# Attention scores on both halves of the partitions, low parts on VectorE, and a matrix of its own for leftover rows

## The chip, the cores and the metric

The kernel runs on one core of a Trainium2 chip. The metric is device time in microseconds (us) of one execution. TensorE (PE) does the matmuls; its weight loads are listed apart as PEld. VectorE is DVE, ScalarE is ACT, GpSimd is POOL, and SyncE (SP) only issues DMAs here.

## The reference

Three layers in a row, in float32, with batch 8, 8 heads, 576 rows, head size 64, 32 memory slots, model width 512 and MLP width 1024:

```python
# attention over a memory of 32 slots, per batch and head
a = softmax(phi, axis=2)                      # 576 x 32
k_m, v_m = a.T @ k, a.T @ v                   # 32 x 64
attn = softmax(q @ k_m.T / 8)                 # the scores: 576 x 32
x = heads_side_by_side(attn @ v_m)            # 576 x 512

# first MLP, with a token shift
x_prev = x shifted down by one row
xk, xr = mu_k*x + (1-mu_k)*x_prev, mu_r*x + (1-mu_r)*x_prev
x = sigmoid(xr @ w_r) * (relu(xk @ w_k)**2 @ w_v)

# second MLP, with a spatial gate
h = relu(x @ w_in); u, v = h[:, :512], h[:, 512:]
v_s = w_spatial @ layer_norm(v) + b_spatial[:, None]
out = (u * v_s) @ w_out
```

The weights reach the kernel as the bits of 64-bit floats and are turned into float32 on the chip.

## The kernel before

**Precision.** Every operand of a large matmul is split into a high part of a shorter float type (an ACT copy) and a low part (a subtraction), and a product is three products: high by high, low by high, high by low (`three`, `gemm`, the matmul at line 95). `split` does it with ACT and DVE (lines 102 and 103); `load_f64`, which brings in a weight chunk, converts its bits (lines 117 to 134) and then splits it with ACT and POOL (lines 140 and 141). A chunk is 128 partitions by 1024 words, 512 KB. The scores alone are plain float32 matmuls, of two instructions each.

**Attention.** `att_step(i)` handles four heads of one batch, so there are 16 steps. A step normalises phi with the transposed maximum (line 222), forms k_m and v_m for the four heads on 32 partitions each (line 233), transposes k_m to 64 partitions (`kmp`, line 267; copied at 268) and computes the scores: for each half of the 576 rows (288, `HB`) a PSUM bank, 4 or 5, with the four heads on 32 output partitions each (line 278). Both operands lie on partitions 0 to 63. A DVE transpose (line 282) takes each half out. Between the halves stands a `yield`. In steps 2 to 15 both halves are normalised together; steps 0 and 1 take one half at a time.

**Order of the work.** The program is written as generators that are advanced by hand. Steps 0 and 1 of attention, the loads and the eight chunks of w_k (`w`) follow the string `ORDER`: A, C, K, Q are phi transposed, phi, keys with values, and queries of step 0; B, D, L, R those of step 1; a lower-case letter is the late half of the queries; `a` and `b` advance the steps; I and M are small constants. Then 16 half batches (`i` in `2 * B`) of the first MLP run; within the first of them `FIRST_BLOCK` brings in the chunks of w_r and w_v. `pump()` after each block of matmuls advances the attention of later batches, and from half batch 14 on `w_in_steps`, which loads w_in and w_out and forms the seven sums that the second MLP's block products use. A tile that is asked for again under the same tag waits until its last reader is done. The compiler's scheduler may start work earlier than its place in the program, but each engine's instructions run in one fixed order, and a DMA waits its turn in SP's queue.

**Between the MLPs.** Each chunk of the first MLP's result is stored to DRAM (`x2d[b]`, line 669) and read back by `load_x2` (lines 553 and 559) as four quarters of 512 rows, whose differences (`minus`, line 548, on POOL) and splits (`put`) feed the second MLP. The products are block products with seven in place of eight (`Group.step`, steps 1, 6, 2, 7, 5, 3, 4): a result is either copied out by ACT (steps 1 and 5, lines 754 and 762) or added by DVE (line 751), and some sums are formed on POOL. `uv(n)` does the u and v products of one batch; as 576 is 512 + 64, the 64 leftover rows of the eight batches are gathered into one more matrix of 512 rows, `uv(B)`. For it `load_x2(B)` reads four pieces from the eight matrices for each quarter. Its steps are advanced by `turn()` during `uv(0)`.

Of the kernel before, what the change touches and what calls it, by code (L numbers as in the profile page):

```python
# [33 lines left out]
ORDER = "AICKMBwwDQwLqwrRaaawaaabbbabaabbwbbwbw"  # L34
# [6 lines left out]
def kernel(  # L41
# [40 lines left out]
    x2d = [dram.tile([128, KC, S], F32, name=f"x2d{b}", tag=f"x2d{b}") for b in range(B)]  # L82
# [25 lines left out]
    def load_f64(src, wh=None, wl=None, raw=None):  # L108
# [32 lines left out]
        nc.gpsimd.tensor_tensor(out=wl, in0=v, in1=wh.bitcast(F32), op=ALU.subtract)  # L141
# [27 lines left out]
    def att_space(f, q, o, n, w, r):  # L169
# [11 lines left out]
        ns.kmT = cut(f, 128)[0:64]  # L181
# [6 lines left out]
        ns.km = cut(n, 64)  # L188
# [10 lines left out]
    def operands(i):  # L199
        b, g = divmod(i, G)  # L200
        sp = space(i)
        return (sp.pT, phiT[b, g]), (sp.ph, phin[b, g]), (sp.kv, kv1[b, g]), (sp.q, qT[b, g])
# [7 lines left out]
    def att_step(i):  # L210
# [30 lines left out]
        nc.vector.tensor_scalar(out=km, in0=kvp[:, 0:64], scalar1=rs, scalar2=None, op0=ALU.mult)  # L241
# [24 lines left out]
        kmp = bank(n_small)[0:64, 0:128]  # L266
# [5 lines left out]
        for halves in ((0,), (1,)) if i < 2 else ((0, 1),):  # L272
            bl = slice(halves[0] * NBLK // 2, (halves[-1] + 1) * NBLK // 2)
            sl = slice(halves[0] * HB, (halves[-1] + 1) * HB)
            for hf in halves:
                sc = bank(4 + hf)[:, 0:HB]
                for j in range(HG):
                    nc.tensor.matmul(  # L278
                        out=sc[32 * j:32 * j + 32, :], lhsT=kmT[:, 32 * j:32 * j + 32],
                        rhs=q[:, j, hf * HB:(hf + 1) * HB], start=True, stop=True,  # L280
                    )
                nc.vector.transpose(
                    out=st[:, hf * NBLK // 2:(hf + 1) * NBLK // 2, :].rearrange("p a m -> p (a m)"), in_=sc
                )
                if hf != halves[-1]:
                    yield True
# [72 lines left out]
    def prep_x(i, which, c):  # L359
# [18 lines left out]
    q0 = q_and_more[0:64, 0:HG * S].rearrange("p (j s) -> p j s", j=HG)  # L378
    q1 = tile_of("kh", [128, HG, S])
    n_r = 2 * HG * 64 + 2 * S  # L380
    rest = q_and_more[:, HG * S:]
    spaces = [
        att_space(
            tile_of("ATh", [128, 4096]), q0, rest[:, 0:2 * S], rest[:, 2 * S:2 * S + 128],
            rest[:, 2 * S + 128:], tile_of("asp", [128, 1792], F32R),
        ),
        att_space(
            tile_of("W3h", [128, 4096]), q1[0:64], tile_of("r", [128, 2 * S]), tile_of("o0", [128, HB]),
# [10 lines left out]
    def load(n, i, late):  # L399
        dst, src = operands(i)[n]  # L400
        if n == 3:
            sl = slice(HB, S) if late else slice(0, HB)
            dst, src = dst[:, :, sl], src[:, :, sl]
# [576 lines left out]
```

## Time and profile before

| | us |
|---|---|
| median of three runs | 1055.05 |
| lowest and highest run | 1052.84, 1057.75 |
| the profiled execution, its own time | 1054.81 |
| span of that execution's trace | 1052.9 |
| PE busy, weight loads busy | 1001.3, 961.1 |
| DVE, ACT, POOL busy | 699.1, 602.5, 150.6 |

The trace holds every instruction of one execution with its engine, start and duration, and what ended the wait before it. All durations and stretches are of this one execution; its time is 1.9 us over the span. Matmuls overlap, so the distance from one start to the next tells their cost, not the duration of one.

### The profile page before, as it was taken

The numbers are of one execution on the slowest core, as the hardware profiler recorded it, in microseconds if no ns is written. First come the engines' busy times: TensorE is split into PE (matmuls) and PEld (weight loads), VectorE is DVE, ScalarE is ACT, GpSimd is POOL, SyncE is SP. The second block draws the span as 40 slices with busy tenths as digits, with TensorE's granted clock in tenths as the row PEclk, the third lists the DMA queues.
The fourth block names the chain that finished last, engine by engine and source line by source line (L and its number), as shares of the span: only waits on it lengthen the run. The fifth ranks groups of instructions, "written<-read, shape, count | busy, mean of one in ns | idle before, by whom it ended". The sixth has DMA issues, their size and how long they took to land.

```text
span 1052.9 us, 20313 instructions
## 1 busy us (share of the span) xinstructions
PE 1001.3 (95%) x8080; PEld 961.1 (91%) x8080; DVE 699.1 (66%) x1534; ACT 602.5 (57%) x1285; POOL 150.6 (14%) x152
## 2 busy tenths in 40 slices
PE   2588999999999999999999998899999999999998
PEld 1386899999999999999999998799999999999998
DVE  5999956655765665566467756886656657574753
ACT  3686865665675567567666662764443535444342
POOL 1333000000000000000011223331222323132220
PEclk9999999999999999999999999999999999999999
DMA  9755523322322232232013222211220111111201
GB/s 277 246 177 160 178 59 107 109 87 57 109 84 77 80 114 82 57 109 87 24 50 106 82 84 63 58 41 41 69 63 30 57 36 52 35 58 37 68 24 45
DMA packets 59614, 88.93 MB, mean 84 GB/s; under 512 B 8960, under 2 KB 52352, under 8 KB 56576
## 3 DMA queue, kind: packets, MB, share of 16 engines
q1 hardware_dynamic: 59520, 87.65, 26.8%
q8 instruction: 63, 1.03, 0.4%
q14 instruction: 31, 0.25, 0.1%
HBM read 68.75 MB, written 18.87 MB: 83 GB/s over the span
## 4 chain that ended last, share of the span: by engine, by line
PE 79%; DVE 7%; issue 5%; DMA 4%; ACT 2%; POOL 2%; SPq 1%; POOLq 0%; DVEq 0%; ACTq 0%
PE bank L95 76%; PE bank L233 1%; PE bank L278 1%; DMA xT<-in_w_k 1%; DMA st<-in_w_in 1%; DVE xs L103 1%; DMA ATh<-in_kv 1%; POOL W1l L141 1%; SPq L553 1%; DVE xT L134 1%; DVE kl L103 1%; DVE st L130 0%; DVE xT L130 0%; DMA st<-in_w_out 0%; DVE W1l L103 0%
## 5 line engine op out<-in xcount | busy, mean ns | idle before, releaser
L95 PE MATMUL bank<-xs,W1h 128*128 128x288 f32 (+1 forms) x1496 | 252.9, 295 | 11.5 <-ACT xs L102 3.7
L95 PEld LDWEIGHTS bank<-xs,W1h 128*128 128x128 f32 x1496 | 214.7, 190 | 17.8 <-ACT xs L102 5.3
L95 PE MATMUL bank<-xs,W1l 128*128 128x288 f32 (+1 forms) x748 | 137.9, 293 | 0.0
L103 DVE TENSOR_TENSOR kl<-t,kh 128x576 fp32r<-128x576 f32 x64 | 51.4, 803 | 103.2 <-ACT kh L102 102.5
L95 PEld LDWEIGHTS bank<-xs,W1l 128*128 128x128 f32 x748 | 112.6, 190 | 0.0
L621 ACT ACTIVATE t<-bank 128x288 f32<-128x288 f32 x128 | 51.1, 402 | 65.9 <-PE bank L95 65.9
L751 DVE TENSOR_TENSOR st<-bank,st 128x256 f32<-128x256 f32 x90 | 37.0, 423 | 73.6 <-PE bank L95 59.8
L95 PE MATMUL bank<-xs,W2h 128*128 128x288 f32 x512 | 84.5, 300 | 0.0
L95 PE MATMUL bank<-kh,W3h 128*128 128x288 f32 x512 | 80.1, 297 | 3.1 <-ACT W3h L140 2.9
L95 PE MATMUL bank<-kh,W3l 128*128 128x288 f32 x512 | 82.5, 299 | 0.4 <-POOL W3l L141 0.3
L95 PEld LDWEIGHTS bank<-kh,W3h 128*128 128x128 f32 x512 | 70.8, 188 | 9.6 <-issue 5.6
L95 PE MATMUL bank<-kl,W3h 128*128 128x288 f32 x512 | 78.4, 295 | 0.0
L95 PEld LDWEIGHTS bank<-kh,W3l 128*128 128x128 f32 x512 | 72.1, 190 | 6.7 <-issue 5.6
L95 PE MATMUL bank<-ATh,xs 128*128 128x256 f32 x472 | 75.1, 282 | 0.8 <-ACT st L754 0.8
L95 PEld LDWEIGHTS bank<-xs,W2h 128*128 128x128 f32 x512 | 72.6, 188 | 2.8 <-ACT t L621 2.2
L95 PEld LDWEIGHTS bank<-kl,W3h 128*128 128x128 f32 x512 | 71.5, 189 | 0.5 <-issue 0.5
L95 PEld LDWEIGHTS bank<-ATh,xs 128*128 128x128 f32 x472 | 64.6, 191 | 1.4 <-ACT st L754 1.2
L103 DVE TENSOR_TENSOR xs<-st,xs 128x512 fp32r<-128x512 f32 x56 | 51.6, 922 | 15.2 <-ACT xs L102 15.2
L102 ACT ACTIVATE xs<-st 128x512 fp32r<-128x512 f32 x56 | 34.0, 629 | 44.0 <-POOL st L548 33.8
L102 ACT ACTIVATE kh<-bank 128x288 fp32r<-128x288 f32 x64 | 25.9, 407 | 51.3 <-DVE bank L871 51.3
L321 POOL MEMSET xT<- 128x4 f32 x8 | 0.8, 106 | 356.8 <-DVE x32b L368 352.3
L892 ACT ACTIVATE o<-bank 128x288 f32<-128x288 f32 x64 | 25.9, 404 | 45.4 <-PE bank L95 35.1
(242 smaller groups left out, 2251.6 us busy)
## 6 DMA issues: line engine op xcount, KB each, us to landing
ATh<-in_kv SPq DMA_DIRECT2D x15, 1300.0 KB, 6.3
x2d<-o SPq DMA_DIRECT2D x64, 144.0 KB, 1.9
out_T<-o SPq DMA_DIRECT2D x64, 144.0 KB, 1.7
st<-x2d SPq DMA_DIRECT2D x32, 256.0 KB, 3.1
ATl<-in_qT SPq DMA_DIRECT2D x14, 576.0 KB, 5.3
ATh<-in_phin SPq DMA_DIRECT2D x15, 320.0 KB, 3.2
ATh<-in_phiT SPq DMA_DIRECT2D x15, 288.0 KB, 2.8
st<-in_w_in SPq DMA_DIRECT2D x8, 512.0 KB, 3.8
```

Of the source, the lines that this page charges most:

```text
L95: nc.tensor.matmul(out=out, lhsT=pairs[i][0], rhs=pairs[i][1], start=i == 0, stop=i == n - 1)
L102: nc.scalar.activation(out=h, in_=x, func=ACTF.Copy)
L103: nc.vector.tensor_tensor(out=lo, in0=x, in1=h.bitcast(F32), op=ALU.subtract)
L134: nc.vector.scalar_tensor_tensor(out=out, in0=top, scalar=3, in1=low, op0=ALU.logical_shift_left, op1=ALU.bitwise_or)
L141: nc.gpsimd.tensor_tensor(out=wl, in0=v, in1=wh.bitcast(F32), op=ALU.subtract)
L233: nc.tensor.matmul(out=kvp[32 * j:32 * j + 32, :], lhsT=ph[:, t, 32 * j:32 * j + 32], rhs=kv[:, t, j, :], start=(t == 0), stop=(t == NT - 1),)
L278: nc.tensor.matmul(out=sc[32 * j:32 * j + 32, :], lhsT=kmT[:, 32 * j:32 * j + 32], rhs=q[:, j, hf * HB:(hf + 1) * HB], start=True, stop=True,)
L321: nc.gpsimd.memset(xT[b][:, :, 0:1], 0.0)
L553: nc.sync.dma_start(out=dst[:, :, 64 * e:64 * e + 64], in_=x2d[4 * half + e][:, 2 * k:2 * k + 2, 2 * HALF:],)
L621: nc.scalar.activation(out=ks[:, m % 2 * HB:(m % 2 + 1) * HB], in_=acc, func=ACTF.Relu)
L751: engine.tensor_tensor(out=dst, in0=x, in1=y, op=ALU.add)
L892: nc.scalar.activation(out=o, in_=acc, func=ACTF.Copy)
```

## The change

- Scores: the queries of row half 0 lie on partitions 0 to 63, those of half 1 on partitions 64 to 127. k_m is written twice side by side before its transpose, so that it stands on both partition halves. The score matmuls of both halves are issued together, head by head and half by half, before the `yield`; the transposes stay on their two sides of it. The queries come in two DMAs.
- `load_f64` forms the low part on DVE in place of POOL.
- `ORDER`: the loads D, L, Q and R come before all but one of the `w`.
- `w_in_steps` starts after half batch 12 and loads the first half of w_in first; the part that needs attention's tiles waits for a flag that is set after half batch 13.
- Leftovers: a matrix `x2r` of its own in DRAM; in the second half of a batch each chunk is stored by two DMAs, and `load_x2(B)` reads each quarter with one. Its differences are formed on DVE, and the ACT instructions of its splits are put behind the latest result copy of `Group.step` in ACT's order (`tc.issue_after`, which sets an order and no wait).

```diff
-from contextlib import ExitStack
+from contextlib import ExitStack, nullcontext
 from types import SimpleNamespace
...
-ORDER = "AICKMBwwDQwLqwrRaaawaaabbbabaabbwbbwbw"
+ORDER = "AICKMBDwLQRwwqwraaawaaabbbabaabbwbbwbw"
...
     eps = tile_of("eps", [128, 1])
-    x2d = [dram.tile([128, KC, S], F32, name=f"x2d{b}", tag=f"x2d{b}") for b in range(B)]
+    x2r = dram.tile([128, KC, B, S - 2 * HALF], F32, name="x2r", tag="x2r")
+    x2d = [dram.tile([128, KC, 2 * HALF], F32, name=f"x2d{b}", tag=f"x2d{b}") for b in range(B)]
...
         nc.scalar.activation(out=wh, in_=v, func=ACTF.Copy)
-        nc.gpsimd.tensor_tensor(out=wl, in0=v, in1=wh.bitcast(F32), op=ALU.subtract)
+        nc.vector.tensor_tensor(out=wl, in0=v, in1=wh.bitcast(F32), op=ALU.subtract)
...
         ns.pT = cut(f, S)
-        ns.kmT = cut(f, 128)[0:64]
+        ns.kmT = cut(f, 128)
         at[0] = 0
...
         at[0] = 0
-        ns.km = cut(n, 64)
+        ns.km = cut(n, 128)
         ns.mx, ns.rs = cut(n, 1), cut(n, 1)
...
         sp = space(i)
-        return (sp.pT, phiT[b, g]), (sp.ph, phin[b, g]), (sp.kv, kv1[b, g]), (sp.q, qT[b, g])
+        qs = [(sp.q[64 * hf:64 * hf + 64], qT[b, g][:, :, hf * HB:(hf + 1) * HB]) for hf in range(2)]
+        return (sp.pT, phiT[b, g]), (sp.ph, phin[b, g]), (sp.kv, kv1[b, g]), *qs
...
         nc.vector.reciprocal(out=rs, in_=rs)
-        nc.vector.tensor_scalar(out=km, in0=kvp[:, 0:64], scalar1=rs, scalar2=None, op0=ALU.mult)
+        nc.vector.tensor_scalar(
+            out=km.rearrange("p (e d) -> p e d", e=2), in0=kvp[:, None, 0:64].to_broadcast([128, 2, 64]),
+            scalar1=rs, scalar2=None, op0=ALU.mult,
+        )
         if wide:
...
         yield False
-        kmp = bank(n_small)[0:64, 0:128]
+        kmp = bank(n_small)[:, 0:128]
         nc.tensor.transpose(out=kmp, in_=km, identity=ident_sb)
...
             sl = slice(halves[0] * HB, (halves[-1] + 1) * HB)
+            scs = {hf: bank(4 + hf)[:, 0:HB] for hf in halves}
+            for j in range(HG):
+                for hf in halves:
+                    nc.tensor.matmul(
+                        out=scs[hf][32 * j:32 * j + 32, :],
+                        lhsT=kmT[64 * hf:64 * hf + 64, 32 * j:32 * j + 32],
+                        rhs=q[64 * hf:64 * hf + 64, j, :], start=True, stop=True,
+                    )
             for hf in halves:
-                sc = bank(4 + hf)[:, 0:HB]
-                for j in range(HG):
-                    nc.tensor.matmul(
-                        out=sc[32 * j:32 * j + 32, :], lhsT=kmT[:, 32 * j:32 * j + 32],
-                        rhs=q[:, j, hf * HB:(hf + 1) * HB], start=True, stop=True,
-                    )
                 nc.vector.transpose(
-                    out=st[:, hf * NBLK // 2:(hf + 1) * NBLK // 2, :].rearrange("p a m -> p (a m)"), in_=sc
+                    out=st[:, hf * NBLK // 2:(hf + 1) * NBLK // 2, :].rearrange("p a m -> p (a m)"),
+                    in_=scs[hf],
                 )
...
     q_and_more = tile_of("ATl", [128, 4096])
-    q0 = q_and_more[0:64, 0:HG * S].rearrange("p (j s) -> p j s", j=HG)
-    q1 = tile_of("kh", [128, HG, S])
+    q0 = q_and_more[:, 0:HG * HB].rearrange("p (j s) -> p j s", j=HG)
+    q1 = tile_of("kh", [128, HG, HB])
     n_r = 2 * HG * 64 + 2 * S
-    rest = q_and_more[:, HG * S:]
+    rest = q_and_more[:, HG * HB:]
     spaces = [
         att_space(
-            tile_of("ATh", [128, 4096]), q0, rest[:, 0:2 * S], rest[:, 2 * S:2 * S + 128],
-            rest[:, 2 * S + 128:], tile_of("asp", [128, 1792], F32R),
+            tile_of("ATh", [128, 4096]), q0, rest[:, 0:2 * S], rest[:, 2 * S:2 * S + 256],
+            rest[:, 2 * S + 256:], tile_of("asp", [128, 1792], F32R),
         ),
         att_space(
-            tile_of("W3h", [128, 4096]), q1[0:64], tile_of("r", [128, 2 * S]), tile_of("o0", [128, HB]),
+            tile_of("W3h", [128, 4096]), q1, tile_of("r", [128, 2 * S]), tile_of("o0", [128, HB]),
             tile_of("o1", [128, HB]), tile_of("W3l", [128, n_r], F32R),
...
     def load(n, i, late):
-        dst, src = operands(i)[n]
-        if n == 3:
-            sl = slice(HB, S) if late else slice(0, HB)
-            dst, src = dst[:, :, sl], src[:, :, sl]
+        dst, src = operands(i)[n + late]
         nc.sync.dma_start(out=dst, in_=src)
...
         chunks = w_in.bitcast(U32).rearrange("(c p) f -> p c f", p=128)
-        room = tile_of("asp", [128, 1792])
...
+        quads = tile_of("xT0", [128, 2, KC, HALF])
+        for half in range(2):
+            for j in range(2):
+                load_f64(part(0, half, j), raw=quads[:, half, :, 128 * j:128 * j + 128])
+                yield
+                yield
+        while not att_free:
+            yield
+        room = tile_of("asp", [128, 1792])
         parts_of("AT", wi_v)
...
             add(raw[:, 2], a11, a21)
-            for q, a in ((0, a11), (1, a12), (2, a22)):
+            for q, a in ((0, a11), (1, a12), (2, a22), (3, raw[:, 0]), (4, raw[:, 1]), (5, raw[:, 2])):
                 split(a, h[:, q], lo[:, q])
-            yield
-            for q, n in ((3, 0), (4, 1), (5, 2), (6, 0)):
-                if q == 6:
-                    add(raw[:, 0], a12, raw[:, 1])
-                split(raw[:, n], h[:, q], lo[:, q])
-            yield
-        quads = tile_of("xT0", [128, 2, KC, HALF])
-        for half in range(2):
-            for j in range(2):
-                load_f64(part(0, half, j), raw=quads[:, half, :, 128 * j:128 * j + 128])
-                yield
+                if q % 2:
+                    yield
+            add(raw[:, 0], a12, raw[:, 1])
+            split(raw[:, 0], h[:, 6], lo[:, 6])
+            yield
         a11, a12, a21, a22 = (quads[:, half, 2 * k:2 * k + 2] for half in range(2) for k in range(2))
...
     x2s = {}
-    w1_free, xT_free, late_free = [], [], []
+    w1_free, xT_free, att_free, late_free = [], [], [], []
...
         def minus(out, a, b):
-            nc.gpsimd.tensor_tensor(out=out, in0=a, in1=b, op=ALU.subtract)
+            engine = nc.vector if rest else nc.gpsimd
+            engine.tensor_tensor(out=out, in0=a, in1=b, op=ALU.subtract)
...
             if rest:
-                for e in range(4):
-                    nc.sync.dma_start(
-                        out=dst[:, :, 64 * e:64 * e + 64],
-                        in_=x2d[4 * half + e][:, 2 * k:2 * k + 2, 2 * HALF:],
-                    )
+                src = x2r.rearrange("p c b s -> p c (b s)")
+                nc.sync.dma_start(out=dst, in_=src[:, 2 * k:2 * k + 2, half * HALF:(half + 1) * HALF])
             else:
...
             ts[q] = place(q)
-            split(x, *ts[q])
+            with tc.issue_after(copied[0].ins) if rest else nullcontext():
+                split(x, *ts[q])
...
-    xs_free = []
+    xs_free, copied = [], [None]
     x2_steps = iter(())
...
             nc.vector.tensor_tensor(out=x2, in0=acc, in1=r[:, m, :], op=ALU.mult)
-            nc.sync.dma_start(out=x2d[b][:, m, hf * HB:(hf + 1) * HB], in_=x2)
+            n = HB if hf == 0 else 2 * HALF - HB
+            nc.sync.dma_start(out=x2d[b][:, m, hf * HB:hf * HB + n], in_=x2[:, 0:n])
+            if hf == 1:
+                nc.sync.dma_start(out=x2r[:, m, b, :], in_=x2[:, n:])
             if not last:
...
             pump()
+        if i == 2 * B - 4:
+            more[0] = w_in_steps()
         if i == 2 * B - 3:
-            more[0] = w_in_steps()
+            for _ in att:
+                pass
+            att_free.append(True)
         if i == 2 * B - 2:
...
             if q == 1:
-                nc.scalar.activation(out=c11, in_=acc, func=ACTF.Copy)
+                copied[0] = nc.scalar.activation(out=c11, in_=acc, func=ACTF.Copy)
             elif q == 6:
...
             elif q == 5:
-                nc.scalar.activation(out=c22, in_=acc, func=ACTF.Copy)
+                copied[0] = nc.scalar.activation(out=c22, in_=acc, func=ACTF.Copy)
                 add(nc.gpsimd, c12, c22, c12)
...
             elif q == 3:
```

## Rows read from the trace of the kernel before

**Rows 1.** The page, part 1: engine, busy us (share of the span), instructions.
```profile
PE 1001.3 (95%) x8080; PEld 961.1 (91%) x8080; DVE 699.1 (66%) x1534; ACT 602.5 (57%) x1285; POOL 150.6 (14%) x152
```

**Rows 2.** Busy time by stretch: stretch, its length, then the columns named.
```profile
core 0: us, PE busy (x) PEld busy (x) DVE busy (x) ACT busy (x) POOL busy (x), PEclk, DMA share, GB/s
0.00:50.00 50.00, 19.50 (x140) 11.71 (x140) 36.67 (x70) 24.83 (x48) 11.66 (x13) 1.00 0.86 255
50.00:100.00 50.00, 41.61 (x306) 37.99 (x307) 48.97 (x89) 38.49 (x79) 16.45 (x12) 0.97 0.57 180
100.00:541.50 441.50, 441.04 (x3728) 415.11 (x3727) 279.46 (x605) 288.29 (x611) 1.57 (x8) 1.00 0.28 88
541.50:575.50 34.00, 33.76 (x255) 33.52 (x254) 26.58 (x52) 24.19 (x57) 7.52 (x8) 1.00 0.25 77
575.50:608.50 33.00, 31.16 (x233) 30.69 (x232) 22.24 (x37) 18.33 (x40) 6.16 (x4) 1.00 0.39 115
...
641.50:691.60 50.10, 42.96 (x338) 41.33 (x337) 35.61 (x89) 28.68 (x63) 17.61 (x19) 0.97 0.21 55
```

**Rows 3.** PE in order of time, steady stretch: start, us, line, out<-in, count.
```profile
163.97 0.69 PE L95 MATMUL bank<-kh,W3l 128*128 128x288 f32 x4
164.59 0.69 PE L278 MATMUL bank<-ATl,ATh 64*32 64x288 f32 x8
165.21 0.79 PE L95 MATMUL bank<-kh,W3l 128*128 128x288 f32 x4
165.85 1.22 PE L95 MATMUL bank<-kl,W3h 128*128 128x288 f32 x8
```

**Rows 4.** PE in order of time, a step with both groups side by side.
```profile
109.41 0.83 PE L95 MATMUL bank<-xs,W1h 128*128 128x288 f32 x5
110.17 1.17 PE L278 MATMUL bank<-ATl,ATh 64*32 64x288 f32 x16
111.27 0.40 PE L95 MATMUL bank<-xs,W1h 128*128 128x288 f32 x1
```

**Rows 5.** Groups of instructions, 100 to 541: count, busy us, mean ns, idle before.
```profile
L267 PE MATMUL bank<-ident,ATl 128*64 128x128 f32 x13 | 3.5, 271 | 0.0
...
L222 PE MATMUL bank<-ident,ATl 128*128 128x128 f32 x12 | 3.3, 276 | 0.0
```

**Rows 6.** Line 291, 0 to 60: ns min/median/max, first and last start.
```profile
L291 DVE TENSOR_TENSOR ATl<-ATl x2: 437/899/1361, 20.3 to 34.9; 128x288 f32<-128x288 f32 x2
```

**Rows 7.** DVE in order of time, low parts of w_out.
```profile
637.70 1.28 DVE L103 TENSOR_TENSOR W2l<-xT,W2h 128x512 fp32r<-128x512 f32 x2
```

**Rows 8.** PE in order of time, the start, with the wait ahead.
```profile
23.29 2.40 PE L233 MATMUL bank<-W3h 128*32 128x130 f32 x40 [4.05 <-DMA W3h<-in_kv]
...
48.11 1.33 PE L95 MATMUL bank<-xs,W1h 128*128 128x288 f32 x4 [3.08 <-ACT xs L102]
```

**Rows 9.** DMA issues: count, KB each, median us from issue to landing.
```profile
x2d<-o SPq DMA_DIRECT2D x64, 144.0 KB, 1.9
...
st<-x2d SPq DMA_DIRECT2D x32, 256.0 KB, 3.1
...
xT<-x2d SPq DMA_DIRECT2D x16, 64.0 KB, 2.3
```

**Rows 10.** SP's queue in order of time, end of the first MLP.
```profile
647.20 0.41 SPq L669 DMA_DIRECT2D x2d<-o  x1
647.65 2.00 SPq L553 DMA_DIRECT2D xT<-x2d  x4
```

**Rows 11.** PE in order of time, first blocks of the second MLP.
```profile
657.95 0.50 PE L95 MATMUL bank<-xs,W1h 128*128 128x256 f32 x2 [2.09 <-DVE st L751]
...
666.90 0.64 PE L95 MATMUL bank<-ATh,kh 128*128 128x256 f32 x4
...
677.33 0.74 PE L95 MATMUL bank<-ATh,kl 128*128 128x256 f32 x4 [1.78 <-DVE st L751]
```

**Rows 12.** ACT in order of time, two places, with the wait ahead.
```profile
578.92 0.69 ACT L122 ACTIVATE st<-st 128x512 f32<-128x512 f32 x1 [6.94 <-DMA st<-in_w_in]
...
655.67 0.63 ACT L102 ACTIVATE kl<-xT 128x512 fp32r<-128x512 f32 x1 [2.68 <-POOL xT L548]
```

## Prediction

> **What bounds the kernel now.** I read the page's engine shares first, then a table of busy time by stretch, then the order of instructions inside the stretches where TensorE rests. TensorE (PE) is busy 1001.3 of 1052.9 us, 95% [rows 1], so 52 us are all that waiting costs. The table says where most of them are [rows 2]: 30.5 us in the first 50, 8.4 us from 50 to 100, 0.5 us in the 441.5 us after that, 1.8 us between 575.5 and 608.5, 7.1 us between 641.5 and 691.6. So from 100 to 541.5 only less TensorE work shortens anything; in the first 100 us and around 642 to 692 the other engines and the transfers decide. From 50 to 100 VectorE (DVE) is busy 48.97 of 50 us: there it is the bound.
>
> **Scores.** Per attention step TensorE runs two groups of eight score instructions (four heads, two instructions each), one group for each half of the 576 rows. In the steady stretch a group stands alone between other matmuls. From the start of the four matmuls ahead of it to the start of the row behind the next four, 1.88 us pass for eight ordinary matmuls and one group; the ordinary ones come every 0.133 us ((1.22 - 0.29)/7 in the last row, 0.29 us being what a lone one lasts), so a group costs 0.81 us and a step 1.62 us [rows 3]. Where the two groups stand next to each other, 111.27 - 109.41 us less five matmuls leaves 1.19 us [rows 4]; the matmuls behind a group run 0.1 us late (0.79 us against the 0.69 us that four last ahead of it, rows 3), so 1.30. The second eight instructions therefore add 0.48 us, 60 ns each, and the fixed part of a group is about 0.3 us.
>
> The change puts each row half on its own 64 partitions of the operand and its own bank, and issues the two halves of a head in turn. Bounds: if the halves stream side by side, a step costs 1.30 - 0.48 = 0.82 us; if one after the other, 1.30. I take 0.85, since the four heads already overlap: eight instructions are done in 0.69 us, where four ordinary ones take as long [rows 3]. Of the 14 steps after the first two, 13 lie behind 100 us, 12 of them separated and one adjacent: before 12 x 1.62 + 1.30 = 20.7 us, after 13 x 0.85 = 11.1. The transpose ahead of the scores grows from 64 to 128 columns; the 128-column one beside it in the program lasts 276 ns against its 271 [rows 5], so 13 x 5 ns, nothing. Gain 9.6 us, at least 20.7 - 16.9 = 3.8, at most 10. As PE rests 0.5 us in all in this stretch, the time shortens one for one.
>
> The Trainium skill speaks against the full gain: "TensorE: Matmul & The Clock Gate", Part 3, reports that packing four row groups gave 3.07 times the speed, not 4. By that share two halves give some 1.5 times, an estimate of 0.96/1.5 + 0.34 = 0.98 us a step and a gain of 8 us in place of 9.6; no run here shows row packing.
>
> The other costs of this part: the km multiply writes twice the columns, and the query load becomes two DMAs of together the same bytes, so SP issues five loads a step in place of four, about 0.4 us of SP's time each (what a store takes there [rows 10]). DVE is busy 279 of 441 us in that stretch and SP has nothing else but stores; both are covered. Without cover a step would pay 0.4 us.
>
> **Low parts on VectorE, and the first loads.** Twenty subtractions of weight low parts (eight chunks of w_k, four of w_r, eight of w_v) run on POOL in the first 101 us. What they cost is seen on DVE: the same 128x288 subtraction takes 437 ns alone and 1361 ns when it meets one [rows 6], 0.92 us more. If nine in ten meet a DVE instruction that has to wait like this, 17 us of DVE's time go. On DVE two such subtractions of weight low parts take 1.28 us, 0.64 each [rows 7]. Cost 20 x 0.64 = 13 us, relief 17: DVE is 4 us better off, and a low part is ready sooner, after 0.64 us and not after what held DVE for 1.36. Bounds: no relief, 13 us more DVE work; or, if all meet, 20 x 0.28 = 6 us less.
>
> The new order of loads moves the second step's exponents and its keys and values (1300 KB) ahead of all but one of the weight chunks (512 KB each). By the shapes, 5.7 MB were asked for up to and with that load, and the matmul that waits for it starts at 23.29 [rows 8]; after, 4.4 MB, at the same rate 17.9 us, so 5.3 us sooner. From there to the first operands of the dense part, for which PE waits at 48.11 [rows 8], the chain runs through DVE, so not all 5.3 arrives. Eight of the meetings lie in that time, 8 x (0.9 x 0.92 - 0.64) = 1.5 us; of the 13.3 us that DVE is idle in the first 50 [rows 2] I let earlier data fill 2. That makes 3.5 up to 50, and the other twelve meetings give 2 of their 2.3 us from 50 to 100: 5.5 us. Bounds: 0 (later weight chunks undo it) and 9.
>
> **Second MLP's weights one half batch sooner.** The four loads of the first half of w_in are issued after half batch 12, not 13, so their conversion falls into 541.5 to 575.5, where DVE has 7.4 us free [rows 2]: four loads of three DVE instructions, 0.64 us each by the nearest row [rows 7], are 7.7 us, while the other half's split moves back. It bears on the 1.8 us of 575.5 to 608.5: ScalarE (ACT) sat 6.94 us behind a w_in transfer [rows 12], with result copies queued behind it. I take 1 us; bounds 1.8, and -2 if the full DVE delays a stretch that now has no waits, or the w_out loads block ACT twice.
>
> **Leftovers.** The last 64 rows of every batch are read by 16 DMAs of 64 KB out of eight matrices; SP needs 0.5 us for each (four in 2.00), and the last store of the first MLP goes out among them at 647.20 [rows 10], though that MLP's last product ends at 641.5, the border in rows 2. Four loads follow it, and the last piece lands at about 649.2 + 2.3 = 651.5 [rows 9, 10]. Now four loads remain; the 32 small stores that are added are spread over eight batches, two a chunk, in an SP queue with 33 us for thirteen issues. The last store can leave near 642.6; with 1.9 us to land, 0.5 to issue and 3.1 for 256 KB [rows 9] the last piece is there near 648, 3.5 us sooner. Its differences move from POOL to DVE (0.64 us each by rows 7), and its splits are queued on ACT behind the copies of results. Before, a split waited 2.68 us on ACT for POOL [rows 12] with copies behind it; DVE waited for the split and PE for DVE, 2.09 us, and 1.78 us came later when DVE was behind [rows 11]. What waits behind a copy now are seven splits, whose first reader starts at 666.90 [rows 11]; they have some 15 us, and nothing else reads them. To be had are the 7.1 us and what the lower granted clock costs (0.97 over 50 us, 1.5 us). I take 4.5: the 2.1 of the blocked queue, and 2.4 of the other 6.5, because layer norm, splits and copies of the first blocks still meet on ACT and DVE. Bounds 1 and 8.6.
>
> **Sum.** 9.6 + 5.5 + 1.0 + 4.5 = 20.6 us off the profiled execution's 1054.8, 1034.2; that execution lies 0.2 us under the median of the runs, 1055.05. I forecast 1035. With the page's price for row packing it would be 1036.
>
> **Rivals.** *The halves stream one after the other* (15%): nothing in this trace shows two row groups at once; then 3.8 in place of 9.6, 1041. *The first 100 us give nothing* (14%): DVE is full from 50 on, and weight chunks come later; 1040. *Another wait takes the place of the leftovers'* (14%): the differences now add to DVE, which was behind at 677; 1039. *Alternating the halves breaks the stream* (4%), the case that ends slower: if each switch of half pays the fixed 0.3 us, a step costs 8 x 0.3 + 0.96 = 3.4 in place of 1.62, and 13 x 1.8 = 23 us are lost; with 11 us from the other parts, 1067. It decides from 2.5 us a step on. Against it: separate banks and partitions, and heads that overlap without such a price. Two of the first three together (8%) give 1044 to 1047. The likeliest keeps 45%.
>
> **How the numbers follow.** Its own range is 1028 to 1040. The range 1027 to 1046 goes from nearly all upper bounds together (10 + 9 + 1.8 + 8.6 = 29 us, 1026) to two failures together. A change under 0.5% (5.3 us) can't be told from none here. Faster by more: all but the broken stream and three failures together, 0.89; within: 0.07; slower: 0.04.
>
> **What would show it.** The score instructions of a step in one group of 16 that takes less than 0.95 us of PE's stream, and a steady period shorter by 0.75 us; PE dense from about 45 us; no DVE subtraction stretched threefold before 100; the last leftover piece in place before 649, and less than 4 us of PE's waits from the end of the first MLP to the first spatial product. It would be wrong if scores still cost 1.3 us or more, the start grew, or the same 7 us of waits stood there under other names.

## The result, and the profile after

The changed kernel takes 1039.62 us (median of four runs, 1038.87 to 1042.05) against 1054.40 in the runs beside it: 0.986 of the time, 95% interval 0.983 to 0.989. It is faster, and the forecast of 1035 was 4.6 us too low, with the time inside the range. The profiled execution took 1039.12 us (span 1037.3), 15.6 us of span less than before, where the terms added up to 20.6.

The page's part 1 and the table by stretch, after, to be read beside [rows 1, 2]; the fixed borders no longer fall on the stages behind the first 100 us:

```profile
PE 989.4 (95%) x8080; PEld 957.8 (92%) x8080; DVE 693.3 (67%) x1558; ACT 605.5 (58%) x1287; POOL 117.3 (11%) x128
```
```profile
core 0: us, PE busy (x) PEld busy (x) DVE busy (x) ACT busy (x) POOL busy (x), PEclk, DMA share, GB/s
0.00:50.00 50.00, 21.98 (x146) 13.04 (x147) 32.84 (x75) 25.32 (x50) 0.31 (x5) 1.00 0.92 255
50.00:100.00 50.00, 42.67 (x339) 39.66 (x339) 49.41 (x112) 43.36 (x86) 0.10 (x1) 1.00 0.63 197
100.00:541.50 441.50, 438.82 (x3782) 420.62 (x3781) 286.45 (x620) 294.00 (x625) 4.32 (x10) 1.00 0.29 92
541.50:575.50 34.00, 32.79 (x247) 32.55 (x247) 24.11 (x42) 23.32 (x52) 9.78 (x8) 1.00 0.22 65
575.50:608.50 33.00, 33.00 (x251) 33.00 (x250) 16.48 (x31) 17.28 (x38) 0.00 (x0) 1.00 0.27 83
```

In the first 100 us DVE gets through 187 instructions in 82.3 us of busy time, before 159 in 85.6. To see where the time came from, I marked in TensorE's rows where each stage begins (half batches by their first product with w_k, `bank<-xs,W1h`):

| stage | before, us | after, us | gain |
|---|---|---|---|
| up to half batch 2 | 140.65 | 134.94 | 5.7 |
| half batches 2 to 12 | 401.50 (36.50 each) | 393.08 (35.73 each) | 8.4 |
| half batch 13 | 33.35 | 36.31 | -3.0 |
| half batch 14 | 34.19 | 31.81 | 2.4 |
| half batch 15 | 31.82 | 31.81 | 0.0 |
| second MLP's first product to first spatial product | 50.14 | 47.68 | 2.5 |
| first spatial product to the end | 361.3 | 361.7 | -0.4 |

**Scores.** TensorE in order of time, after, the place that answers to [rows 3]:

```profile
194.14 0.69 PE L96 MATMUL bank<-kh,W3l 128*128 128x288 f32 x4
194.77 0.72 PE L285 MATMUL bank<-ATl,ATh 64*32 64x288 f32 x16
195.41 0.79 PE L96 MATMUL bank<-kh,W3l 128*128 128x288 f32 x4
196.05 0.70 PE L96 MATMUL bank<-kl,W3h 128*128 128x288 f32 x4
```

All 16 instructions last 0.72 us where 8 lasted 0.69. From 194.14 to 196.05, less eight ordinary matmuls of 0.133 us, a step costs 0.85 us; the two groups cost 1.62. From half batch 2 to half batch 12 there are eleven steps, 11 x 0.77 = 8.5 us, the 8.4 of the table.

**Start.** TensorE's rows at the start, answering to [rows 8], and the two-operand subtraction of the score normalisation (line 301), beside [rows 6]:

```profile
19.38 1.91 PE L235 MATMUL bank<-W3h 128*32 128x130 f32 x26 [4.06 <-DMA W3h<-in_kv]
...
36.62 2.79 PE L96 MATMUL bank<-xs,W1h 128*128 128x288 f32 x8 [2.97 <-ACT xs L103]
47.42 1.04 PE L96 MATMUL bank<-xs,W1h 128*128 128x288 f32 x2 [5.61 <-ACT xs L103]
```
```profile
L301 DVE TENSOR_TENSOR ATl<-ATl x2: 451/455/459, 24.0 to 47.2; 128x288 f32<-128x288 f32 x2
```

The keys of step 1 are there 3.9 us sooner (5.3 forecast), no subtraction of this line is stretched, and TensorE's last long wait ends at 47.4, not 45. Nor is any other: of DVE's two-operand instructions in the first 100 us none lasts more than 1.12 times the shortest of its line and shape, where before one of 128x576 took 1609 ns against 741.

**Half batch 13.** TensorE waits for the split of the last attention step's values (line 325), and ACT sits behind w_in transfers; these waits are new:

```profile
531.49 0.79 PE L96 MATMUL bank<-asp 128*128 128x288 f32 x4 [1.71 <-DVE asp L325]
...
551.63 1.32 PE L96 MATMUL bank<-kh,W3h 128*128 128x288 f32 x8 [1.21 <-ACT r L651]
```
```profile
528.35 0.68 ACT L123 ACTIVATE st<-st 128x512 f32<-128x512 f32 x1 [2.37 <-DMA st<-in_w_in]
```

**Leftovers.** The last leftover load leaves SP at 633.37, 5.4 us behind the first product of the second MLP; before, the last four left between 647.65 and 649.65, up to 8.1 us behind it [rows 10]. The waits of [rows 11] are gone and three others stand in their place:

```profile
643.73 0.50 PE L96 MATMUL bank<-xs,W1h 128*128 128x256 f32 x2 [1.13 <-DVE st L767]
...
657.57 0.74 PE L96 MATMUL bank<-ATh,xs 128*128 128x256 f32 x4 [3.07 <-ACT st L770]
...
660.41 0.79 PE L96 MATMUL bank<-kl,W1h 128*128 128x256 f32 x2 [1.15 <-ACT st L778]
661.01 1.05 PE L96 MATMUL bank<-ATh,kl 128*128 128x256 f32 x4
```
```profile
640.00:650.00 10.00, 8.87 (x76) 8.67 (x75) 9.86 (x24) 8.89 (x18) 3.50 (x4) 1.00 0.35 98
```
```profile
650.00:660.00 10.00, 6.20 (x51) 5.75 (x50) 8.64 (x28) 7.67 (x18) 0.96 (x1) 0.95 0.17 52
660.00:670.00 10.00, 9.59 (x60) 9.59 (x61) 6.87 (x20) 4.99 (x11) 2.89 (x4) 0.71 0.01 2
```

The splits and differences of the leftovers, held back by the tie, crowd into 640 to 650, where DVE is busy 9.86 of 10 us. The layer norm of the first four v blocks stands in the same queues. The leftovers' v results are copied (lines 770 and 778) into the two tiles that hold those blocks, so by the program a copy waits for the last split in its tile. In the trace the low part of the third block is formed from 656.35 to 657.04, that of the fourth from 659.19 to 659.88, and the copies start at 657.13 and 659.98. TensorE waits 3.07 and 1.15 us for a bank, and from 660.41 to 665.7 it runs at half clock (granted 0.50): four matmuls in 1.05 us where 0.62 is usual.

### The profile page after: what moved, and what is told of

It reads as the page before. It is cut to its first block, busy times and chain, and to the rows that moved or that the text cites. A ratio compares the mean times of both kernels' runs of the same rounds, so it can differ in the third digit from the quotient of the medians.

```text
span 1037.3 us, 20311 instructions
## 1 busy us (share of the span) xinstructions
PE 989.4 (95%) x8080; PEld 957.8 (92%) x8080; DVE 693.3 (67%) x1558; ACT 605.5 (58%) x1287; POOL 117.3 (11%) x128
## 4 chain that ended last, share of the span: by engine, by line
PE 81%; DVE 9%; DMA 4%; ACT 4%; issue 1%; SPq 1%; POOL 0%; ACTq 0%; POOLq 0%; DVEq 0%
PE bank L96 78%; PE bank L235 2%; DMA ATl<-in_qT 1%; DMA st<-in_w_in 1%; PE bank L285 1%; DVE xs L104 1%; DVE kl L104 1%; DMA ATh<-in_kv 1%; DVE st L131 1%; DVE xT L135 1%; DMA st<-in_w_v 0%; DVE xT L131 0%; ACT st L750 0%; ACT xs L103 0%; POOL st L558 0%
## 5 line engine op out<-in xcount | busy, mean ns | idle before, releaser
L96 PEld LDWEIGHTS bank<-xs,W1h 128*128 128x128 f32 x1496 | 214.4, 190 | 15.1 <-ACT xs L103 10.4
L96 PE MATMUL bank<-xs,W1l 128*128 128x288 f32 (+1 forms) x748 | 136.9, 292 | 0.0
L104 DVE TENSOR_TENSOR kl<-t,kh 128x576 fp32r<-128x576 f32 x64 | 49.1, 767 | 110.4 <-ACT kh L103 109.7
```

Of the source, the lines that this page charges most:

```text
L96: nc.tensor.matmul(out=out, lhsT=pairs[i][0], rhs=pairs[i][1], start=i == 0, stop=i == n - 1)
L104: nc.vector.tensor_tensor(out=lo, in0=x, in1=h.bitcast(F32), op=ALU.subtract)
```

## The experiments

Each kernel is compared with the kernel before on the same chip. Columns: median, ratio with interval; then, of its profiled execution, where half batch 2 starts, where the second MLP starts, the stretch from there to the first spatial product, TensorE's rest in it (stretch less busy time), the granted clock in it, and the time from the first spatial product to the end.

| run | us | ratio | half batch 2 | second MLP | stretch | rest | clock | to the end |
|---|---|---|---|---|---|---|---|---|
| before | 1054.4 to 1056.1 | | 140.65 | 641.51 | 50.14 | 7.14 | 0.97 | 361.3 |
| changed | 1039.62 | 0.986 (0.983 to 0.989) | 134.94 | 627.95 | 47.68 | 5.34 | 0.93 | 361.7 |
| 1 one row group | 1045.18 | 0.991 (0.988 to 0.993) | 137.07 | 635.55 | 46.93 | 4.42 | 0.93 | 361.8 |
| 2 low parts on POOL | 1043.71 | 0.989 (0.987 to 0.991) | 139.22 | 631.97 | 45.00 | 5.06 | 1.00 | 362.5 |
| 3 old order | 1041.27 | 0.986 (0.984 to 0.988) | 136.43 | 630.83 | 47.78 | 5.44 | 0.93 | 361.6 |
| 4 w_in late | 1036.76 | 0.982 (0.980 to 0.985) | 134.80 | 626.74 | 45.56 | 5.68 | 1.00 | 363.6 |
| 5 no matrix of their own | 1040.89 | 0.986 (0.983 to 0.988) | 136.29 | 630.18 | 45.26 | 5.45 | 1.00 | 363.5 |
| 6 differences on POOL | 1042.00 | 0.988 (0.986 to 0.990) | 137.34 | 630.98 | 48.35 | 4.12 | 0.89 | 361.4 |
| 7 no tie | 1041.34 | 0.986 (0.984 to 0.988) | 136.91 | 629.91 | 44.71 | 3.71 | 1.00 | 365.5 |
| 8 spatial splits tied | 1040.31 | 0.986 (0.983 to 0.988) | 137.14 | 631.24 | 46.61 | 3.78 | 0.93 | 363.7 |
| 9 w_in, leftovers as before | 1041.02 | 0.986 (0.984 to 0.988) | 132.62 | 625.27 | 48.33 | 7.01 | 1.00 | 363.6 |
| 10 three edits | 1041.41 | 0.986 (0.985 to 0.987) | 138.55 | 630.46 | 45.65 | 3.15 | 0.96 | 363.9 |
| 11 scores alone | 1044.86 | 0.990 (0.988 to 0.991) | 140.49 | 632.23 | 48.35 | 6.74 | 1.00 | 362.4 |
| 12 w_in late, no tie | 1037.77 | 0.983 (0.982 to 0.985) | 134.19 | 626.02 | 44.66 | 2.36 | 0.96 | 362.8 |

Nine of these executions (changed, 4 to 10, 12) run the same code up to half batch 2 (5 and 9 but for four small stores), and it starts between 132.62 and 138.55, 135.9 on average. They fall apart by the granted clock from 50 to 100 us: the four at 1.00 start at 132.6 to 134.9, the five at 0.90 to 0.97 at 136.3 to 138.6; whether the clock delays the start or a late start lowers the clock is not shown. One execution's start therefore tells little under some 3 us.

The last column must be read with the stretch. Where the stretch is short, TensorE waits once more, some 25 us behind the first spatial product, for a low part of the gated result (line 104): 0.11 us in the changed kernel, 1.64 in run 4, and in run 7

```profile
699.64 0.73 PE L96 MATMUL bank<-ATh,xs 128*128 128x256 f32 x4 [1.67 <-DVE kl L104]
```
with half clock behind it. From the second MLP's first product to the end it is 411.4 us before, 409.4 in the changed kernel, 410.2 in run 7, 411.9 in run 9, 409.2 in run 4 and 407.5 in run 12.

**1. Scores issued together, both halves on partitions 0 to 63** (k_m written once, and the tiles of q and k_m as before; of the diff only the matmul is shown).
```diff
-                        lhsT=kmT[64 * hf:64 * hf + 64, 32 * j:32 * j + 32],
-                        rhs=q[64 * hf:64 * hf + 64, j, :], start=True, stop=True,
+                        lhsT=kmT[:, 32 * j:32 * j + 32],
+                        rhs=q[:, j, hf * HB:(hf + 1) * HB], start=True, stop=True,
```


> The changed kernel (1039.6 us), but with both row halves of the scores on partitions 0 to 63, all 16 instructions of a step still in one group. Theory (the two partition halves stream side by side): the group grows from about 0.7 to 1.2 us of PE's stream, 12 or 13 steps lose 0.48 us each, so some 6 us: 1045.5. Rival (putting the two groups together was the gain, the partitions do nothing): the group stays, the time stays at 1039 to 1040.

```profile
196.59 0.69 PE L96 MATMUL bank<-kh,W3l 128*128 128x288 f32 x4
197.22 1.19 PE L282 MATMUL bank<-ATl,ATh 64*32 64x288 f32 x16
198.34 0.80 PE L96 MATMUL bank<-kh,W3l 128*128 128x288 f32 x4
198.97 0.70 PE L96 MATMUL bank<-kl,W3h 128*128 128x288 f32 x4
```
By the same subtraction a step costs 2.38 - 1.06 = 1.32 us, and the period is 36.20 us: 0.30 less than before for one fixed part saved, and 0.47 more than with two row groups. So putting the groups together gives two fifths of the gain and the second row group the rest; the time is 5.6 us over the changed kernel's. The two halves alternate and go to two banks here too, so neither explains the 0.47.

**2. Low parts back on POOL.**
```diff
-        nc.vector.tensor_tensor(out=wl, in0=v, in1=wh.bitcast(F32), op=ALU.subtract)
+        nc.gpsimd.tensor_tensor(out=wl, in0=v, in1=wh.bitcast(F32), op=ALU.subtract)
```


> The changed kernel, but with the weights' low parts of the first MLP back on POOL. Theory (each POOL subtraction held a DVE instruction for 0.9 us, DVE does it in 0.64): the stretched DVE subtractions come back, the start of half batch 2 moves from 134.9 to 138 or 139 us, and the time to 1043. Rival (the start is set by loads and by the chain through attention, not by DVE's load): half batch 2 starts within 1 us of 134.9 and the time stays at 1039 to 1040.

Half batch 2 starts at 139.22, 4.3 us behind the changed kernel's own execution and 3.3 behind the average of the nine. POOL is busy 28.9 us of the first 100, and line 301 is stretched again (up to 1052 ns, in step 1). The start alone is little outside the scatter, and only 2.0 us behind the five executions with a lowered clock, which this one shares (0.94); the median of six, 1043.7, is what the theory gave.

**3. Old order of loads.**
```diff
-ORDER = "AICKMBDwLQRwwqwraaawaaabbbabaabbwbbwbw"
+ORDER = "AICKMBwwDQwLqwrRaaawaaabbbabaabbwbbwbw"
```


> The changed kernel, but with the old order of the first loads and stages. Theory (the earlier keys and values of step 1 are worth part of their 4 us): the start of half batch 2 moves from 134.9 to 136 or 137 us, the time to 1041. Rival (DVE is full from 31 us on and makes up for any order): within 0.7 us of 134.9 and 1039.6.

The keys of step 1 come 6.6 us later (their product starts at 25.98), yet half batch 2 starts at 136.43, inside the scatter of the nine, and the time can't be told from the changed kernel's. What the order alone is worth is not shown.

**4. The second MLP's weights as before** (loads issued after half batch 13, the conversion's four steps in their old order, of which the diff here shows the first).
```diff
-        if i == 2 * B - 4:
-            more[0] = w_in_steps()
         if i == 2 * B - 3:
-            for _ in att:
-                pass
-            att_free.append(True)
+            more[0] = w_in_steps()
```


> The changed kernel, but with the second MLP's weights brought in as before, from half batch 14 on, the attention tiles' half first. Theory (the earlier start only moved the waits: half batch 13 got 3.0 us longer, half batch 14 2.4 us shorter): 13 takes 33.4 us again, 14 takes 34.2 again, the time stays within 1 us of 1039.6. Rival (the early start is worth the 1.8 us of waits that half batch 14 had, and 13's length has another cause): 14 grows, 13 stays at 36.3, and the time is 1041.5 or more.

Half batches 13 and 14 take 33.33 and 33.58 us, 66.9 together, against 68.1 after the change and 67.5 before it. Undoing this part gains 1.2 us in its place, and the other executions agree: the two half batches take 66.9 to 67.7 us in the five with the old place, 68.0 to 69.2 in the seven with the new one (run 1, with other scores, left out). The time, 1036.76, is the lowest of all kernels, though its interval overlaps the changed kernel's.

**5 to 7. One part of the leftovers undone at a time**: 16 loads from eight matrices (the stores into them are left out of the diff); the differences on POOL; the splits not tied.
```diff
-                src = x2r.rearrange("p c b s -> p c (b s)")
-                nc.sync.dma_start(out=dst, in_=src[:, 2 * k:2 * k + 2, half * HALF:(half + 1) * HALF])
+                for e in range(4):
+                    nc.sync.dma_start(
+                        out=dst[:, :, 64 * e:64 * e + 64],
+                        in_=x2d[4 * half + e][:, 2 * k:2 * k + 2, 2 * HALF:],
+                    )
```
```diff
-            engine = nc.vector if rest else nc.gpsimd
-            engine.tensor_tensor(out=out, in0=a, in1=b, op=ALU.subtract)
+            nc.gpsimd.tensor_tensor(out=out, in0=a, in1=b, op=ALU.subtract)
```
```diff
-            with tc.issue_after(copied[0].ins) if rest else nullcontext():
-                split(x, *ts[q])
+            split(x, *ts[q])
```


> The leftovers are again stored with their rows into the eight matrices and read by 16 transfers of 64-element runs instead of 4 of 256; the subtractions on VectorE and the tie behind the result copies stay. Theory 1 (the matrix of their own is what ended the waits of this stage): the last leftover lands some 10 us after the start of the stage again, behind the tie it can't be split before that, and the second Strassen set waits: the stretch from the first product of this stage to the first spatial product is 2 to 4 us longer than the changed kernel's 47.7, the time 1041.5 to 1043.5. Theory 2 (the tie holds the splits to some 19 us after the start in any case, and 16 transfers land before that): the stretch stays within 0.7 us, the extra store on SP goes, and the time is 1039 to 1040.5.

> Only the four differences of the leftovers go back to POOL. Theory 1 (VectorE is full here, 9.86 of 10 us from 640 to 650, and its queue is what the result additions wait for): VectorE gets back 4 x 0.68 = 2.7 us, the 1.1 us wait of TensorE at 643.7 goes, the two later waits (3.07 and 1.15) shrink with the chain, and the time is 1 to 2.5 us less: 1037 to 1038.5. Theory 2 (the shared port decides): each POOL difference takes some 1.3 us, the next split waits for it and VectorE's two-operand work beside it is stretched: the stretch is 1 to 3 us longer, the time 1040.5 to 1042.5.

> Only the tie of the leftovers' splits behind the result copies goes; matrix of their own and VectorE's differences stay. Theory 1 (the tie is what keeps result copies out from behind splits): the waits of TensorE for result additions and copies come back as before the change (2.09 and 1.78 us), and the stretch to the first spatial product is 2 to 4 us longer than 47.7, the time 1041.5 to 1043.5. Theory 2 (with a matrix of their own the leftovers land by 636, nothing is left for the splits to wait for, and the tie only delays them): no such wait, the splits spread over 636 to 648, the stretch is 0 to 2 us shorter, the time 1037.5 to 1039.5.

Without the matrix the rest is 5.45 us, as in the changed kernel: theory 2's cause, though the stretch, 45.26 us at full clock, is 2.4 shorter and not within 0.7. Without the tie the rest falls to 3.71 and the old waits do not return, so theory 1 is out; but the stretch's 3.0 us come back behind it (365.5 to the end against 361.7), so neither theory held, and that the tie only delays is shown for the stretch, not for the time. The times, 1040.9 and 1041.3, lie 0.4 and 1.8 us above what theory 2 gave; in the profiled executions half batch 2 started later than in the changed kernel's, at 136.3 and 136.9. With the differences on POOL, these last 5.38 us for four in one row, and DVE waits 4.23 us behind them; the stretch grows by 0.7 us, less than theory 2 said, and its clock is lowest, so most of that is clock: the rest is 1.2 us smaller. The time, 1042.0, is inside theory 2's range. None of the three, undone alone, brings the old 7 us back.

**8. The spatial weights' splits tied as well.**
```diff
-            split(x, *ws[t, hf])
+            with tc.issue_after(copied[0].ins):
+                split(x, *ws[t, hf])
```


> The changed kernel, and the splits of the spatial weights tied behind the latest result copy as well (one line). Theory 1 (the new waits of 3.07 and 1.15 us come from the normalisation chain standing in ScalarE's and VectorE's queues between these splits, and the half clock after them from the waits): both waits fall below 1 us together, the granted clock stays at 1.00 from 660 to 670, the stretch to the first spatial product is 3 to 5 us shorter than 47.7, and the time is 1034.5 to 1036.5. Rival (the chain itself, eight steps from engine to engine for each of four tiles, sets them): the waits stay within 1 us of their sum of 4.2, and the time stays at 1038.5 to 1040.5, or is longer because the splits come late for the spatial product.

The two waits fall from 4.22 to 2.65 us (1.86 and 0.79), halfway between the theories: at most 1.6 us of them were the splits'; that the normalisation chain makes the rest is argued, not shown. The granted clock fell all the same, and no gain in time can be told.

**9. Weights and leftovers both as before** (the diffs of runs 4 to 7 in one).

> The scores on both halves, the low parts on VectorE and the order of the first loads stay; the second MLP's weights and everything of the leftovers (their matrix, VectorE's differences, the tie) are as before the change. It stands beside the run with the weights alone as before (span 1035.9, 45.56 us from the first product of the second MLP to the first spatial product, at full clock). Theory 1 (the parts of the leftovers do the same thing twice, so that each alone can be taken away free, but not all): the waits of rows 11 come back, that stretch is 48.5 to 50.2 us, and the time is 1039 to 1041.5. Theory 2 (the leftovers' part is worth nothing, and that stretch differs between kernels by the granted clock alone): 45 to 46.5 us at full clock, the time 1036 to 1038.5.

The stretch is 48.33 us, 0.2 short of theory 1's range and 1.8 above theory 2's, with 7.01 of rest; the time, 1041.0, is inside theory 1's range. At full clock this is 2.8 us more than run 4, and to the end both take 363.6, so the gain stays. The old waits on line 759 (the result additions) are back:

```profile
641.57 0.51 PE L95 MATMUL bank<-xs,W1h 128*128 128x256 f32 x2 [1.46 <-DVE st L759]
643.53 0.51 PE L95 MATMUL bank<-xs,W1h 128*128 128x256 f32 x2 [0.28 <-DVE st L759]
645.04 0.50 PE L95 MATMUL bank<-xs,W1h 128*128 128x256 f32 x2 [0.54 <-ACT xT L762]
646.92 0.50 PE L95 MATMUL bank<-xs,W1h 128*128 128x256 f32 x2 [0.91 <-ACT xT L762]
...
660.89 0.73 PE L95 MATMUL bank<-ATh,kl 128*128 128x256 f32 x4 [1.66 <-DVE st L759]
```

**10 and 12. Towards a better kernel**: both have the diff of run 4 and that of run 7's tie; run 10 also has that of run 8.

> The changed kernel without two of its parts and with one line more: the second MLP's weights as before, no tie of the leftovers' splits, and the spatial weights' splits tied behind the latest result copy. If the gains seen one at a time add (about 3 for the weights, 0.3 for the tie, 1 for the spatial weights), the stretch from the second MLP's first product to the first spatial product is 43.5 to 45 us at full clock and the time is 1033.5 to 1036. Rival: the tie of the spatial weights only moves the wait (their splits then stand in front of the next result copies), and the time is that of the weights alone as before, 1036 to 1038.

> The changed kernel with the second MLP's weights as before and without the tie of the leftovers' splits; the spatial weights' splits as in the changed kernel. It stands beside the run that ties those too. Theory 1 (the normalisation chain behind these splits costs about 1 us): the stretch is 44.5 to 45.5 us at full clock, the time 1035.5 to 1037, 0.7 to 1.5 us over the run with both. Theory 2 (the chain itself sets it): the two are within 0.4 us.

Run 12 has the smallest rest, 2.36 us, and 1037.77 us, 0.983 of before; runs 4 and 12 are the two kernels ahead of the changed one, by 1.9 to 2.9 us in the median. Run 10 lost 3.6 us to run 12, against both its theories and both of run 12's. Of the 6.5 us between their profiled executions 4.4 lie ahead of half batch 2, where their code is the same, and 2.1 behind the second MLP's start; but the other three of run 10, whose mean granted clock was 0.995 to 0.998, took 1040.2 to 1041.6 as well. Why stays open.

**11. The kernel before with the scores alone** (the diffs of runs 2, 3 and 4 to 7 on the changed kernel).

> The kernel before with the scores on both row halves alone. Theory: 13 steps in the dense stretch give 0.8 us each, the first hundred us and the last stretches keep the waits they had before: the period falls from 36.50 to 35.7, 9.5 to 11 us in all, the time 1043.5 to 1045.5. Rival (the scores' gain depends on the low parts having left POOL, or on the new order of loads): 0 to 6 us, the time above 1048.

Half batch 2 starts at 140.49, as before the change (140.65), the period is 35.73, and the second MLP starts 9.3 us sooner. The time is 11.2 us less in the median. The theory held.

## Why the prediction was right, and where its sizes were off

- **Scores: right.** 0.85 us a step was forecast and measured, against 1.62 [rows 3]; the period fell by 0.77 us. "Side by side" is shown by run 1, and 9.6 us by run 11 (9.3 at the second MLP's start). The Trainium skill's figure ("TensorE: Matmul & The Clock Gate", Part 3: four row groups, 3.07 times) had given an estimate of 0.98 us a step. Here the second row group took off 1.32 - 0.85 = 0.47 us, all but 0.01 of what the second eight instructions cost; less the fixed part of 0.34, streaming fell from 0.96 to 0.51 us, 1.9 times where the share had given 1.5.
- **Low parts and first loads: right in kind, a third too large.** 5.5 forecast. In the trace 5.7; against the average start of the nine, 140.65 - 135.9 = 4.8. Some 1.2 us of either are the scores', for two steps lie between 100 us and half batch 2 (one of separated groups, 0.77, and the adjacent one, 0.45); that leaves 3.6, and the medians, from run 11 to run 9, give 3.8. Run 2 puts 2.0 to 3.3 us on the low parts (3.5 forecast). The step that failed is the 2 us that the earlier keys were to bring on to the dense part: run 3 shows no gain from them. The step from 23.29 to 17.9 for the keys was also too much, since with one code this load came at 17.4 in one execution and at 19.4 in another. And of the eight meetings counted behind the keys two lie ahead of them: POOL's subtractions at 16.68 and 20.05.
- **Second MLP's weights: wrong in sign.** The step "I take 1 us" failed. The 6.94 us of ACT behind a w_in transfer did go; three waits behind w_out transfers, of 4.0 us at most, came, and TensorE has no wait in half batch 14, which gained 2.4 us (0.75 of them come with the scores alone, run 11). But half batch 13 lost 3.0, because the conversion met the last attention step and the result copies on ACT and DVE. Run 4 prices the part at 1.2 us lost. My lower bound, -2 "if the full DVE delays a stretch that now has no waits", named this case.
- **Leftovers: mechanism partly right, size too large.** 4.5 forecast; 2.5 in the trace, 2.8 at full clock (runs 9 and 4). The blocked queue went as said, but without the tie it stays away too (run 7), and the matrix of their own is not needed if the rest stays (run 5). The rival "another wait takes the place" came true in part: rest fell from 7.14 to 5.34 us, not under 4. The step that failed is the 2.4 us taken of the other 6.5: what stands there now is the copy into tiles that the first v blocks still hold, 3.07 and 1.15 us, and the half clock behind it, 0.93 over the stretch.
- **The sum.** In the trace the terms are 9.6 for the scores (8.4 and the 1.2), 3.6 for the start, -0.6 for half batches 13 and 14 against before, and 2.5 for the leftovers: 15.1, against 15.6 in the span. Of the 5.5 us missing from 20.6, the start is 1.9, the weights 1.6 and the leftovers 2.0. In the medians, before, run 11, run 9, run 4 and the changed kernel form a chain, one part more at each step; their ratios, 1, 0.990, 0.986, 0.982 and 0.986, make steps of about 11, 4, 4 and -4 us, the last three uncertain by some 3 each. The time is inside the range because the scores, two thirds of the gain, were right; every other term was too large.

## What to carry to other kernels

Matmuls of half the row depth can be had nearly free in pairs, if the two operands lie on different partition halves (here the results also went to different banks; whether that is needed no run shows); look for the place where TensorE is the bound, as each us saved there counts. Work moved sooner must be read against the engine queues of the stage that it lands in: a transfer wait that cost 1.8 us was exchanged for 3.0 us of blocked attention and result copies. Before a split is tied behind other work, look at whether its data is there anyway by then; a tie that ends no wait only bunches work. And follow a gain to the end of the program: run 7's shorter stretch was paid back by a wait 25 us further on.

## What the runs showed of the hardware

TensorE's clock did not fall to its lower level, 1.2 GHz, after every wait of the same size. In run 4 TensorE rested 3.40 and 1.16 us and then ran at 2.4 GHz; in run 12 it rested 1.80 us, and the next matmuls ran at half of that:

```profile
656.77 0.74 PE L96 MATMUL bank<-ATh,xs 128*128 128x256 f32 x4 [3.40 <-ACT st L764]
659.61 0.50 PE L96 MATMUL bank<-kl,W1h 128*128 128x256 f32 x2 [1.16 <-ACT st L772]
```
```profile
654.81 1.09 PE L96 MATMUL bank<-ATh,xs 128*128 128x256 f32 x4 [1.80 <-ACT st L764]
655.70 0.63 PE L96 MATMUL bank<-ATl,xs 128*128 128x256 f32 x2
```

In the changed kernel's execution the clock took 0.29 x 9.59 = 2.8 us of TensorE's work from 660 to 670. The start shows the same: with the same code, run 4 (first) had full clock from 30 to 50 us and run 10 (second) half:

```profile
30.00:40.00 10.00, 6.38 (x28) 3.23 (x27) 9.48 (x22) 8.46 (x17) 0.00 (x0) 1.00 0.67 221
40.00:50.00 10.00, 4.38 (x16) 3.81 (x17) 10.00 (x22) 7.08 (x15) 0.00 (x0) 1.00 0.92 291
```
```profile
30.00:40.00 10.00, 6.78 (x28) 3.63 (x28) 8.68 (x21) 8.68 (x18) 0.00 (x0) 0.50 0.73 229
40.00:50.00 10.00, 4.00 (x14) 3.43 (x15) 10.00 (x22) 7.27 (x16) 0.00 (x0) 0.50 0.91 290
```

Half clock there does not make a late start by itself. Run 9 had it too, and of the nine executions with this code its half batch 2 starts first (132.62), that of run 10 last (138.55):

```profile
30.00:40.00 10.00, 5.98 (x24) 3.65 (x22) 9.97 (x24) 8.91 (x19) 0.00 (x0) 0.50 0.70 233
40.00:50.00 10.00, 4.78 (x23) 4.64 (x24) 10.00 (x22) 7.50 (x17) 0.00 (x0) 0.57 1.06 349
```
TensorE is busy 4 to 7 us of 10 there and DVE nearly 10, so TensorE isn't the bound. From 50 to 100, where it is busy 42.6 and 42.7 us, run 9 was granted 1.00 and run 10 0.90.

So stretches of different executions are compared here by TensorE's rest and granted clock, not by their length alone.
